# Another written-out order for all engines in a fused attention and feed-forward kernel

## The chip, the cores and the metric

One core of one Trainium2 chip runs the kernel. The metric is the device time of one execution in microseconds (us). TensorE is called PE here, ScalarE ACT, VectorE DVE, GpSimd POOL and SyncE SP, as in the profile.

## The reference, cut to what matters

Attention over 4 batches, 8 heads, 768 positions and 64 values per head. Some heads ("retrieval", three of eight here) see every earlier position; the others ("streaming") see the first 4 positions and a window of 64. Its result, 3072 tokens by 512, goes through a two-layer block with the activation h - tanh(h).

```
scores = q @ k.T / 8;  scores = where(mask, scores, -1e9)     # mask: causal, and per head full or sink + window
a = softmax(scores);   x = (a @ v), heads side by side         # x: 3072 x 512
h = x @ w_in                                                   # w_in: 512 x 2048
out = (h - tanh(h)) @ w_out                                    # w_out: 2048 x 512
```

Inputs and output are fp32; the kernel computes in fp16 with fp32 accumulation.

## The kernel before, in words

The tokens are cut into 12 tiles of 256 (`TT`); three tiles make a batch. A tile has four head pairs. For tile t and pair p the steps are: **T** t.p, four PE transposes that turn q and k of the pair (`st_T`, L1242), whose copies out of PSUM fill `QK` (L1222 on ACT, L1224 on DVE); **S**, the score products (`st_S`, L1367), numbered through by their PSUM area; **exp** on ACT (L1386); **mask pt**, a product on DVE (L1423); **A** t.p, the product with v (`st_A`, L1451); **rinv** and **x16**, reciprocal and scaling on DVE (L1471, L1512); **X** t.p, two PE transposes (L1547) and the copy **xT**. Tile 0 takes its masks as extra products ahead of S (**add**, L1340 and L1343). From tile 3 on, the transposes of q, k and x are done by DMA on SP's queue (`turn`, L750; `st_X_tile`, L1529), after POOL has gathered the heads in the order of their kind (`gather`, L848 and L884).

The second part runs in units. **H** t.u multiplies the tile's x by two column blocks of w_in (`H_unit`, L1598); units 0 and 1 need part 0 of w_in, 2 and 3 part 1, 4 and 5 part 2, 6 and 7 part 3. **th** t.u is the tanh on ACT (L1612), **gt** t.u the subtraction on DVE (L1623). **O** multiplies by w_out (L1671), from tile 4 on in a form with seven half-sized products instead of eight (`piece`, L1797), for which sums of operands are made on DVE or POOL (`sums`, L1764; `add`, L1868; `combine`).

For the early masks and products with far v, `masks` (L1094) and `scale_v` (L940: v times a per-head flag, one 128-row block of v each, called scale_v0 to scale_v3 for tile 0 and 1) make tables; `by_head` (L1082) makes the diagonal matrices for **add**; `by_rank` computes where each head goes, ending in `perm`, which POOL and DVE read into registers (`get`). The other loads of the start: `load_first` asks for q and k of tile 0, each in two halves of four heads, `cast_first` turns them into fp16; `load_cast(1)` brings q and k of tile 1 as fp16 through POOL's queue, and four **move** copies order them; `load_v`, `load_w_in` and `load_w_out` go through POOL's queue too, which casts on the way.

What sets the order: every operation is registered once with `P.op` in a fixed numbering, with its reads and writes. The list `SEQ`, written out in the source, is the order in which they are then issued; each engine gets its own operations in that order and works strictly in turn. `BANK` gives each PSUM user its bank. `SIZE` gives the lengths of filler matmuls (L2138: products of a matrix of ones, whose results nobody reads) that stand in PE's order at the start. `TE`, `XE`, `CASTS`, `IE`, `SUMS`, `ADDS`, `TAKES`, `SVS` and `OE` say which of two engines does a given copy, cast, sum or product.

```
for i in self.seq[a:b]:
    self.ops[i][2]()                     # Plan.follow: issue in the order of SEQ
```

Of the kernel before, what the change touches and what calls it, by code (L numbers as in the profile page):

```python
# [118 lines left out]
]  # L119
SIZE = {128: 20, 129: 17, 130: 7, 131: 6, 132: 3, 133: 11, 134: 6}  # L120


class Plan:
# [259 lines left out]
def kernel(  # L383
# [97 lines left out]
    XE = ('ADDA', 'AAAD', 'DADA')  # L481
# [6 lines left out]
    CASTS = ('AA', 'AD')  # L488
# [1828 lines left out]
```

## Time and profile before

| | |
|---|---|
| time, median of 3 runs | 222.72 us (222.02, 222.72, 224.2) |
| span of the profiled execution | 221.4 us; its whole time is not given beside it |
| PE busy | 212.2 us (96%) |
| DVE, ACT, POOL busy | 182.4, 136.2, 137.8 us |
| filler matmuls | 70, 6.6 us of PE's busy time |
| TensorE clock granted | 0.996 of full speed |

The span runs from the first to the last instruction of the program; the time of a run is a little longer. In a row of the timeline the columns are start, duration, engine, line, operation, tiles written and read, shape and count; brackets hold the idle time before it and what ended it. In a row of the windows, each engine has its busy time and its count of instructions in that stretch.

### The profile page before, as it was taken

The page shows a single profiled execution, that of the slowest core. Times are in us where ns is not written, and L with a number is a line of the kernel's source. Part 1 is how long each engine was busy: PE and PEld are TensorE (multiplying, and loading weights), DVE is VectorE, ACT ScalarE, POOL GpSimd, SP SyncE. Part 2 cuts the span into 40 slices and gives each one's busy share as a digit, 9 for nine tenths or more (in the row PEclk, how much of TensorE's full clock was granted, in tenths as well). Part 3 has the DMA queues.
Part 4 walks back from the last instruction along what each step waited for, and adds up shares of the span by engine and source line. Part 5 has one row for each costly group of instructions (what it writes and reads, how often), then busy time and mean ns, then how long its engine had stood idle before and what let it go on. Part 6 is the DMA issues. An engine that isn't in the chain of part 4 may idle for free. (4 is left out here: it accounts for less than half of the span.)

```text
span 221.4 us, 6599 instructions
## 1 busy us (share of the span) xinstructions
PE 212.2 (96%) x2485; PEld 175.6 (79%) x2485; DVE 182.4 (82%) x456; ACT 136.2 (62%) x223; POOL 137.8 (62%) x267
## 2 busy tenths in 40 slices
PE   7789999999999999999999999999999999999990
PEld 7467898788887576877887988989888888888880
DVE  5799976565959699899999999997887897786871
ACT  3779767995365869666475668546456865634510
POOL 8981993950757668489995798977985020071330
PEclk9999999999999999999999999999999999999998
DMA  6999999999999999999999988938137032022023
GB/s 174 172 197 206 144 177 157 191 235 190 199 200 218 239 192 201 217 193 256 209 266 202 213 160 171 236 63 132 49 69 172 3 95 98 3 47 96 3 96 104
DMA packets 112743, 34.56 MB, mean 156 GB/s; under 512 B 98882, under 2 KB 112194, under 8 KB 112706
## 3 DMA queue, kind: packets, MB, share of 16 engines
q1 hardware_dynamic: 86896, 26.75, 58.9%
q0 software_dynamic: 24992, 6.82, 30.2%
q10 hardware_dynamic: 818, 0.52, 0.8%
q8 instruction: 20, 0.33, 0.6%
q14 instruction: 17, 0.14, 0.2%
HBM read 27.26 MB, written 6.29 MB: 152 GB/s over the span
## 5 line engine op out<-in xcount | busy, mean ns | idle before, releaser
L1598 PE MATMUL banks<-xT,win 128*128 128x256 f16 x768 | 95.4, 273 | 0.1
L1612 ACT ACTIVATE th<-banks 128x512 f32<-128x512 f32 x96 | 55.4, 604 | 45.6 <-PE banks L1598 42.1
L1598 PEld LDWEIGHTS <-win 128*128 128x128 f16 x768 | 72.6, 98 | 11.7 <-issue 1.4
L1623 DVE SCALAR_TENSOR_TENSOR gt<-th,banks 128x512 f16<-128x512 f32 x88 | 58.0, 680 | 9.2 <-ACT th L1612 8.2
L1386 ACT ACTIVATE pt<-banks 128x1024 f16<-128x1024 f32 (+3 forms) x57 | 49.9, 911 | 6.4 <-PE banks L1367 6.1
L848 POOL CAST t<-rawqk 128x256 f16 x64 | 27.0, 448 | 15.6 <-DMA rawqk<-in_k_dram 10.4
L1797 PEld LDWEIGHTS <-m 128*128 128x128 f16 x256 | 24.4, 98 | 3.3 <-issue 0.4
L1671 PE MATMUL banks<-wout,gt 128*128 128x256 f16 (+1 forms) x160 | 26.1, 294 | 0.0
L884 POOL CAST v<-rawv 128x128 f16 x64 | 20.5, 350 | 6.8 <-DMA rawv<-in_v_dram 6.6
L1497 DVE TENSOR_TENSOR x16t<-banks,rinv 128x128 f32 (+1 forms) x80 | 22.9, 288 | 1.5
L1386 ACT ACTIVATE ptn<-banks 128x1024 f16<-128x1024 f32 (+1 forms) x18 | 17.2, 954 | 10.3 <-PE banks L1367 10.1
L1868 POOL TENSOR_TENSOR ot<-gu,ot 128x256 f32<-128x256 f32 x9 | 6.7, 744 | 24.5 <-ACT gu L1836 20.6
L1367 PE MATMUL banks<-QK 64*128 64x128 f16 (+1 forms) x343 | 21.1, 236 | 0.4 <-ACT pt L1386 0.3
L1797 PEld LDWEIGHTS <-gt 128*128 128x128 f16 x192 | 18.2, 98 | 2.9 <-issue 0.3
L1367 PEld LDWEIGHTS <-QK 64*128 64x128 f16 x343 | 13.0, 94 | 7.3 <-issue 6.1
L1451 PEld LDWEIGHTS <-pt 128*128 128x128 f16 x390 | 16.4, 97 | 1.7 <-issue 0.5
L1797 PE MATMUL banks<-wout,gt 128*128 128x256 f16 x128 | 17.8, 273 | 0.0
L1797 PE MATMUL banks<-wout,m 128*128 128x256 f16 x128 | 17.6, 273 | 0.0
L1671 PEld LDWEIGHTS <-gt 128*128 128x128 f16 x160 | 14.1, 98 | 3.9 <-issue 0.3
L1451 PE MATMUL banks<-v,pt 128*128 128x65 f16 x208 | 16.4, 193 | 0.0
L1471 DVE RECIPROCAL rinv<-banks 128x4 f32<-128x4 f32 x48 | 8.2, 175 | 7.0 <-PE banks L1451 6.9
L1423 DVE TENSOR_TENSOR pt<-pt,m4r 128x1024 f16<-128x1024 f16 (+1 forms) x18 | 12.7, 707 | 1.5 <-ACT pt L1386 1.3
(129 smaller groups left out, 324.6 us busy)
## 6 DMA issues: line engine op xcount, KB each, us to landing
rawqk<-in_q_dram SPq DMA_DIRECT2D x18, 256.0 KB, 4.3
out_dram<-ot SPq DMA_DIRECT2D x18, 256.0 KB, 2.6
rawqk<-in_k_dram SPq DMA_DIRECT2D x17, 256.0 KB, 4.3
rawv<-in_v_dram SPq DMA_DIRECT2D x16, 256.0 KB, 4.3
win<-in_moe_w_in_dram POOLq DMA_DIRECT2D x4, 512.0 KB, 8.9
wout<-in_moe_w_out_dram POOLq DMA_DIRECT2D x4, 512.0 KB, 9.4
out_dram<-ot SPq DMA_DIRECT2D x10, 128.0 KB, 4.1
v<-in_v_dram POOLq DMA_DIRECT2D x6, 128.0 KB, 6.7
```

The source lines that it names most:

```text
L848: nc.gpsimd.tensor_copy(out=c5()[:, :, :, s_ : s_ + 1, :], in_=r5()[:, :, :, at, :])
L884: nc.gpsimd.tensor_copy(out=v1s[b]()[:, g * NB : g * NB + NB, RANK[s_] : RANK[s_] + 1, 0:D], in_=rw()[:, :, at, :],)
L1367: nc.tensor.matmul(out=flat[:, 512 * hh + o : 512 * hh + o + nb * 128], lhsT=lhsT, rhs=QK[p_, hp, q_0 : q_0 + nb * 128], start=not added, ...
L1386: nc.scalar.activation(out=o_, in_=i_, func=AF.Exp, scale=inv_sqrt_d)
L1423: nc.vector.tensor_mul(out=pv, in0=pv, in1=m)
L1451: nc.tensor.matmul(out=av()[:, i, hh, :], lhsT=pt()[:, hh, co : co + 128], rhs=vv, start=(jb == first_jb[hh]), stop=(jb == qb),)
L1497: nc.vector.tensor_mul(out=xt()[:, :, at, :], in0=av()[:, :, hh : hh + 1, 0:D], in1=rinv()[:, :, hh : hh + 1].unsqueeze(3).to_broadcast([1 ...
L1598: nc.tensor.matmul(out=ph()[:, j, :], lhsT=w_in_t[fb // 4][:, cb, f0 : f0 + 128], rhs=xT()[:, :, cb, :], start=(cb == 0), stop=(cb == HP - 1),
L1612: lambda: nc.scalar.activation(out=th()[:], in_=ph()[:], func=AF.Tanh, scale=1.0 / XS),
L1623: nc.vector.scalar_tensor_tensor(out=o_, in0=a, scalar=-XS, in1=b, op0=ALU.mult, op1=ALU.add,)
L1671: nc.tensor.matmul(out=po()[:, c0:c1], lhsT=gt()[:, f, ts * 128 : ts * 128 + 128], rhs=w_out_t[:, f, c0:c1], start=(f == 0), stop=(f == NF ...
L1797: nc.tensor.matmul(out=po()[:, at : at + CM], lhsT=lhs(c), rhs=rhs(c), start=c == 0, stop=c == NC - 1,)
```

## The change

The arithmetic is the same. The numbers in `SEQ` stand in another order, `BANK` fits it, three fillers are left of seven, and 67 operations change their engine.

```diff
 SEQ = [
-    0, 1, 14, 7, 2, 4, 16, 10, 17, 3, 15, 5, 8, 6, 13, 18, 9, 19, 12, 57,
...
+    1, 3, 7, 15, 14, 4, 5, 6, 8, 9, 12, 13, 0, 18, 19, 128, 20, 10, 57, 37, 38, 21, 22, 49, 30, 35, 31,
...
-SIZE = {128: 20, 129: 17, 130: 7, 131: 6, 132: 3, 133: 11, 134: 6}
+SIZE = {128: 21, 129: 23, 130: 3}
-    TE = (('AA', 'AD', 'AD', 'AA'), ('AA', 'AA', 'DD', 'AA'), ('AA', 'AA', 'DD', 'DA'))
-    XE = ('ADDA', 'AAAD', 'DADA')
+    TE = (('AD', 'AA', 'DD', 'DA'), ('AA', 'DD', 'DA', 'AA'), ('AA', 'DA', 'DD', 'DD'))
+    XE = ('DDDA', 'DDAA', 'DADA')
-    CASTS = ('AA', 'AD')
+    CASTS = ('DA', 'AD')
-    SUMS = ('DDDDDDDD', 'DDDDDDDD', 'DDDDDDDD', 'DDDDDDDD', 'DDDDPPDP', 'PDDDDPDD', 'DDPDDDPP', 'DDDPDDPP', 'PDPDDPDP', 'DDDDDPDD', 'PDDDDPDD', 'DDPDDDDD')
+    SUMS = ('DDDDDDDD', 'DDDDDDDD', 'DDDDDDDD', 'DDDDDDDD', 'DDDDDPPP', 'DDDDPPPP', 'PDDDPPDP', 'DPPDPDPD', 'PDPDDPDP', 'PDDDPDDP', 'DPPPDDPD', 'DDDDDDPD')
...
-    SVS = ('PP', 'PP')
+    SVS = ('DD', 'DP')
-    IE = (('AD', 'DA'), ('DA', 'DA'))
+    IE = (('DD', 'DA'), ('DA', 'DA'))
-    OE = ('ADAD', 'AADD', 'AAAA', 'AAAA', 'AAAA', 'AAAA', 'AAAA')
+    OE = ('AAAA', 'DDDA', 'AAAA', 'AAAA', 'AAAA', 'AAAA', 'AAAA')
```

`ADDS` and `TAKES` change likewise. Read by names, the orders begin so (the two lists of an engine hold the same work, shifted):

```
SP before    load q half 0, load q half 1, load k half 0, two stores among raw loads of tile 4, turn 3, ...
SP after     load k half 0, load q half 0, load q half 1, two stores, turn 3, raw loads of tile 4, turn 3, ...
ACT before   load k half 1, cast q half 0, cast k half 0, cast q half 1, six QK copies, exp0, move, exp1, exp2, exp3, move
ACT after    load k half 1, cast k half 0, cast q half 1, q0.0, q0.1, k0.1, exp0, k0.3, exp1, exp2, move, exp3
POOL before  ..., load t1 q, v block 1, v block 0, load t1 k, v block 3, w_in 0, v block 2, w_in 1, w_in 2,
             scale_v0, table mS, scale_v3, scale_v1, w_in 3, table mS, registers (perm), w_out 0.0, tile 2, ..., w_out 0.1
POOL after   ..., load t1 q, v block 0, v block 1, load t1 k, w_in 0, w_in 1, v block 2, v block 3, w_in 2,
             tables mS, w_in 3, scale_v3, w_out 0.0, w_out 0.1, tile 2, tile 3, registers (perm), last q of tile 3, ...
DVE after    ..., by_head x4, cast q half 0, cast k half 1, by_head, k0.0, by_head, thr, mask, by_head, move, q0.2, k0.2, by_head,
             move, mask, q0.3, rinv0.0, x16 0.0, rflag0, move, mask, rinv0.1, rinv0.2, x16 0.1, xT0.0, x16 0.2, rinv0.3, x16 0.3,
             xT0.2, xT0.1, scale_v1, mask, q1.2, mask, k1.1, mask, q1.1, mask pt4, scale_v0, gt0.1, gt0.0, ..., by_rank spread to perm
PE before    fill x20, flags, fill x17, add 0, fill x7, T0.1, T0.0, T0.2, T0.3, fill x6, S 0, add 1, S 1, ..., S 3, A0.1, fill x3,
             X0.0, A0.2, T1.0, A0.2, A0.3, fill x11, X0.1, T1.3, T1.2, T1.1, X0.2, X0.3, fill x6, S 4, H0.0 and H0.1 in part, S 6
PE after     fill x21, flags, fill x23, T0.0, T0.1, add 0, T0.2, S 0, add 1, T0.3, S 1, A0.0, add 2, S 2, ..., S 3, X0.0, A0.2, T1.0,
             T1.3, fill x3, A0.3, X0.1, X0.2, T1.2, X0.3, T1.1, S 4, H0.0 and H0.1 whole, S 6
```

(S 0 to S 3 are tile 0; S 4, 6, 8 and 10 are the four pairs of tile 1, each with two PSUM areas, of which the second number is left out.)

In the diff's later part the order is shuffled for every engine to the end of the kernel: on SP the DMA transposes of tiles 4 to 8 stand at the same place or up to five places earlier, and loads of raw v stand later. The last seven operations of PE and the last six stores are the same.

More of the change, by code (lines that the diff above doesn't have):

```diff
@@ L499 @@
     STEPL = {1: (1, 4), 4: ('a',), 6: (2, 6, 'e'), 7: (5, 'b', 3, 7, 'f')}
-    SUMS = ('DDDDDDDD', 'DDDDDDDD', 'DDDDDDDD', 'DDDDDDDD', 'DDDDPPDP', 'PDDDDPDD', 'DDPDDDPP', 'DDDPDDPP', 'PDPDDPDP', 'DDDDDPDD', 'PDDDDPDD', 'DDPDDDDD')
-    ADDS = ('PPP', 'PPP', 'PPP', 'PPP', 'DDP', 'PDP', 'DPP', 'PPD', 'PPD', 'PPD', 'PPP', 'PPP')
-    TAKES = ('AA', 'AA', 'AA', 'AA', 'AA', 'DA', 'AA', 'AA', 'AA', 'AA', 'AA', 'AA')
-    SVS = ('PP', 'PP')
+    SUMS = ('DDDDDDDD', 'DDDDDDDD', 'DDDDDDDD', 'DDDDDDDD', 'DDDDDPPP', 'DDDDPPPP', 'PDDDPPDP', 'DPPDPDPD', 'PDPDDPDP', 'PDDDPDDP', 'DPPPDDPD', 'DDDDDDPD')
+    ADDS = ('PPP', 'PPP', 'PPP', 'PPP', 'PPD', 'PPD', 'PPD', 'DDP', 'PPD', 'DPP', 'DPP', 'PPP')
+    TAKES = ('AA', 'AA', 'AA', 'AA', 'AA', 'DD', 'AD', 'AA', 'AA', 'AA', 'AD', 'AA')
+    SVS = ('DD', 'DP')
     HINT = (11, 1, 0)
```

200 rows, old and new, of tables (BANK, SEQ) are left out of this document.

## The prediction, made before the changed kernel was run

> **What bounds the kernel now.** I read the page first, then PE by stages, then the timeline of the first 30 us, then the landings of single transfers.
>
> ```profile
> span 221.4 us, 6599 instructions
> PE 212.2 (96%) x2485; PEld 175.6 (79%) x2485; DVE 182.4 (82%) x456; ACT 136.2 (62%) x223; POOL 137.8 (62%) x267
> PE   7789999999999999999999999999999999999990
> ```
>
> PE is the only engine near its span, so the next question is where it isn't busy, or busy with nothing.
>
> ```profile
> 0.00:17.40 17.40, 13.82 (x177) 10.81 (x177) 13.29 (x43) 11.38 (x25) 14.63 (x27) 1.00 1.37 182
> 17.40:25.00 7.60, 7.32 (x103) 6.00 (x102) 7.25 (x23) 7.49 (x13) 3.90 (x6) 1.00 1.13 176
> 25.00:215.00 190.00, 189.70 (x2200) 157.93 (x2199) 160.00 (x387) 117.28 (x187) 118.63 (x234) 1.00 0.88 155
> 215.00:221.40 6.40, 1.36 (x13) 0.91 (x10) 1.82 (x7) 0.00 (x0) 0.68 (x2) 0.87 0.28 91
> L2138 PE MATMUL banks<-ones 128*128 128x128 f16 x70 | 6.6, 263 | 1.2 <-POOL ones L976 1.2
> PE banks L1367 <- DMA QK<-t: 0.2, 1, 0.2
> ```
>
> The windows give span, then busy time of PE, weight load, DVE, ACT, POOL. From 25 to 215 us PE is busy 189.70 of 190.00 us; its only wait there is 0.2 us. Nothing can be won there, only lost. The last 6.40 us hold the last results and stores, whose order is unchanged. What is left is the head: of its 17.4 us PE works 13.82, and 6.6 of these are fillers. So 10.2 us of the head (17.4 - 13.82 + 6.6) do nothing useful, and the change is worth what it takes from these, as far as PE stays fed afterwards. In the head I followed what each wait ended on:
>
> ```profile
> 3.91 0.62 ACT L1222 CAST t<-rawqk 128x512 f16<-128x512 f32 x1 [0.95 <-DMA rawqk<-in_q_dram]
> 5.99 0.43 DVE L1224 CAST t<-rawqk 128x512 f16<-128x512 f32 x1
> 6.87 1.14 ACT L1222 CAST t<-rawqk 128x512 f16<-128x512 f32 x2 [2.33 <-DMA rawqk<-in_k_dram]
> 7.54 1.14 PE L1242 MATMUL banks<-ident,t 128*128 128x128 f16 x14 [1.42 <-ACT t L1222]
> 8.38 0.45 DVE L1224 COPY QK<-banks 128x256 f16<-128x256 f16 x1 [1.36 <-ACT QK L1222]
> 9.69 0.87 ACT L1386 ACTIVATE pt<-banks 128x768 f16<-128x768 f32 x1
> 10.23 2.18 DVE L1094 TENSOR_SCALAR m<-A,thr 128x512 f16<-128x512 f16 x2
> 11.14 1.11 POOL L940 TENSOR_TENSOR vf<-v,rflag 128x520 f16<-128x520 f16 x1
> 12.70 2.11 POOL L940 TENSOR_TENSOR vf<-v,rflag 128x520 f16<-128x520 f16 x2
> 12.87 1.02 DVE L1224 COPY t<-t16p 128x512 f16<-128x512 f16 x1
> 15.88 0.42 DVE L1512 TENSOR_TENSOR x<-banks,rinv 128x256 f16<-128x256 f32 x1
> 17.41 1.50 PE L1598 MATMUL banks<-xT,win 128*128 128x256 f16 x12
> 18.34 0.35 DVE L1094 TENSOR_SCALAR m<-A,thr 128x512 f16<-128x512 f16 x1
> 18.85 0.56 PE L1367 MATMUL banks<-QK 64*128 64x256 f16 x10
> ```
>
> ACT waits 2.33 us for the first half of k, and PE 1.42 us behind it. From 8.38 us on DVE is the bound: it never rests, and it is slowed by POOL. A mask takes 0.35 us alone (18.34), but two take 2.18 where POOL's scale_v starts at 11.14, and a move takes 1.02 beside the scale_v of 12.70. The last x is ready at 16.3 us (15.88 + 0.42), the first H runs at 17.41.
>
> **The change part by part.** *k first.*
>
> ```profile
> L628 SPq DMA_DIRECT2D rawqk<-in_q_dram x1: 505/505/505, 1.4 to 1.4; - x1
> DMA to landing us min/median/max: 4.0/4.0/4.0
> rawqk<-in_k_dram ACTq DMA_DIRECT2D x1, 256.0 KB, 4.4
> ```
>
> SP's three loads land at 3.9, 5.4 (1.4 + 4.0) and 6.8 us; each wait above ended on one. They are of one size, so I give the same three times to k half 0, q half 0, q half 1. k half 1 on ACT's queue stays at 5.9 (5.99, cast). The first pair's transposes need q and k of half 0: 5.4 + 0.43 for DVE's cast is 5.9 us, against 7.54. But the cast of q half 1 stands on ACT ahead of the copies q0.0, q0.1, k0.1, so these wait for 6.8 + 0.6 = 7.5 us. exp0 then starts at about 8.4, against 9.69: of 1.6 us won at the transposes, 1.3 are left.
>
> *DVE's chain.* From its cast at 5.5 us to the last copy of x (xT0.1) DVE has 29 pieces in the new order: 2 casts and 5 QK copies of 0.43-0.45, 4 x16 of 0.42, 3 masks and 3 moves of 0.35 (bounds for a move 0.35 and 1.02; I take the low end, since no POOL product runs beside them), some 12 small ones of 0.16-0.3. That is about 9.5 us, less some overlap, plus waits for exp and PSUM: the end falls at 14.5 us, and at 15.5 if POOL's DMA issues slow the masks and moves. scale_v0 and scale_v1 now come behind that, on DVE. The trace has no such product on DVE; the nearest row above is POOL's 1.1, and a mask of 128x512 at 0.35 bounds it below; I take 0.7, in the middle. First H at 15.1 us (15.0 to 16.3).
>
> *What is late next.* The second S of tile 1 (18.85 above) waits for scale_v1, three masks and three QK copies that stand on DVE between xT0.1 and it: 0.7 + 3 x 0.35 + 3 x 0.43 = 3.0 us less overlap, so 17.1 us instead of 18.85. Ahead of it PE now does 16 H products instead of 12; four at 0.125 (1.50 for 12) are 0.5 more. **Lead there: 1.75 + 0.5 = 2.2 us**, or 0.3 if DVE's chain ends at its late bound and every piece after it is slowed too.
>
> *w_in sooner.*
>
> ```profile
> L815 POOL DMA_DIRECT2D win<-in_moe_w_in_dram x1: 780/780/780, 10.4 to 10.4; - x1
> DMA to landing us min/median/max: 10.7/10.7/10.7
> 22.35 1.16 PE L1598 MATMUL banks<-xT,win 128*128 128x256 f16 x9
> ```
>
> Part 2 is asked for at 10.4 and lands at 21.1, after 10.7 us of queue. Ahead of it stand the same eight loads as before, in another order. Parts 0 and 1 pass two blocks of v and come sooner, in time for 15.1 and 17.6; part 2 I leave at 21.1. PE would want it at 20.7 and waits 0.4. Its first use was at 22.35, and 0.66 us of H and X that stood behind it are now done before: **lead 1.25 + 0.66 = 1.9 us**.
>
> *w_out.*
>
> ```profile
> 21.10 0.90 POOL L826 DMA_DIRECT2D wout<-in_moe_w_out_dram  x1 [5.22 <-DVE gt L1623]
> L826 POOL DMA_DIRECT2D wout<-in_moe_w_out_dram x1: 902/902/902, 21.1 to 21.1; - x1
> DMA to landing us min/median/max: 6.2/6.2/6.2
> 28.21 0.38 PE L1671 MATMUL banks<-wout,gt 128*128 128x256 f16 x2
> ```
>
> Before, POOL stood 5.22 us at its register load ahead of w_out; part 0.0 landed at 27.3 (21.1 + 6.2), first use 28.21. The register load now stands behind 10 more DMAs, so POOL asks once v block 3 has landed and scale_v3 is done, near 19.8. Bounds: 26.0 (the same 6.2) and 27.3 (the queue as full as before). PE with its lead wants it at 26.6, and part 0.1, some 3 us behind it, at 29.8. Loss 0 to 1.1 us; I take 0.2, nearer the low end, since the 6.2 is the shortest wait of the large loads shown. **Lead 1.7 us.** The registers come late; POOL's gathers of tile 3 need raw data that land at 39 us, so 31 is early enough.
>
> *Keeping it to 215 us.*
>
> ```profile
> 84.82 2.90 SPq L1529 DMA_TRANSPOSE xT<-x16t  x1
> xT<-x16t SPq DMA_TRANSPOSE x1, 4.9
> 89.72 0.50 PE L1598 MATMUL banks<-xT,win 128*128 128x256 f16 x3
> ```
>
> This x landed at 89.7 (84.82 + 4.9) and PE used it at 89.72: no slack. A lead of 1.7 us lives on only if such transposes come 1.7 us earlier. In SP's new order this one has 37 operations ahead instead of 41, and those of tile 7 have 55 instead of 58; at 0.5 to 0.6 us for an issue that is about 2 us. Raw loads of v stand later for it, as tile 7 to 9 need them late. The moves between DVE and POOL cost nothing by themselves: from 25 us on DVE is busy 160.00 and POOL 118.63 of 190. Bounds: 0 and the whole lead. I take 0.
>
> *Fillers* are 47 instead of 70, in time that was idle.
>
> **Sum:** 221.4 - 1.7 = 219.7 us of span. The median of the runs stands 1.3 above the span of the profiled execution (222.72 - 221.4), which I keep: **221.0 us**. Less than 1%, 2.2 us, is about what can't be told from no change here.
>
> **Rivals.**
>
> *The whole lead arrives* (0.30): the queue isn't as full as I hold it, part 2 of w_in and w_out land with the earlier asking, and 2.2 to 3 us stay: 219.5 to 220.5, say 220.1. For it: part 0 of w_out, asked alone, took 6.2 us where part 2 of w_in took 10.7. Against it: the bytes ahead of part 2 are the same.
>
> *The lead is given back* (0.12): the x of tile 4 or the gathers behind more sums on POOL don't come sooner, PE waits there instead; 222.2, between 221.7 and 223.2. For it: slack zero at 89.72; against: those transposes were moved forward.
>
> *Slower* (0.11): POOL's register load waits for perm, whose small steps stand on DVE between eight subtractions of 0.7 us; behind it stand the last q of tile 3, v, and part 1.0 of w_out, which gates all later raw loads. Near 31 us it costs nothing. Each microsecond beyond moves tile 3 and then SP's whole queue; with the 1.7 us of lead used up at 34, a perm at 36.5 gives 225.2. Against it: DVE is, by the sum above, some 2 us ahead of its old pace then.
>
> *The clock* (0.05). Fillers ran before PE's real work, and there are 23 fewer in a head with gaps.
>
> ```profile
> 1.15 2.31 PE L2138 MATMUL banks<-ones 128*128 128x128 f16 x20 [1.15 <-POOL ones L976]
> 14.38 0.78 PE L2138 MATMUL banks<-ones 128*128 128x128 f16 x11
> ```
>
> The first twenty start 0.1 us apart (2.31 for 20), eleven later ones 0.06 (0.78 less 0.2 of drain); so PE speeds up on the way, though the granted clock reads 1.00 throughout, and it stayed fast over its 1.42 us of idling before 7.54. If the new gaps let it fall back to half pace for about 3 us of work, 1.5 us go: 222.5. The Trainium skill, page "TensorE: Matmul & The Clock Gate", section "What's actually happening", says that PE runs at half clock until a window of about 3.4 us was busy and falls back after an idle one. By that rule the new head, whose longest pause I put at 0.6 us, stays fast; the rows agree, and no run here shows a fall.
>
> A second rule speaks against the change: by the page "DMA: Bandwidth & Descriptors" of the Trainium skill, section "SWDGE vs HWDGE vs iDMA", POOL writes its descriptors into SBUF, from which DVE's two-port modes lock it out. A busier DVE beside POOL's ten issues would then make them later. [...]
>
> **How the numbers follow.** Forecast 0.42: 220.5 to 221.7, at 221.0. The rivals have 0.30, 0.12, 0.11 and 0.05. Faster by over 1% (under 220.5) is the whole lead and a little of the forecast's edge: 0.34. Slower by over 1% (over 224.9) is the register case: 0.10. The rest, 0.56, is within. The range runs from the low end of the whole lead, 219.5, past lead given back, to 223.4; it leaves out the slower case and some 0.05 below.
>
> **What would show it.** T0.0 near 6 us, exp0 near 8.4, first H near 15.1 with no wait for w_in, the S behind it at 17.1, waits of PE for win near 21 and for wout near 27, fillers 47, PE's busy time from 25 to 215 still over 189. I am wrong if masks and moves stay slow without POOL's products (then H starts after 16.3), if PE waits over 1 us in all between 25 and 215, or if POOL's register load ends after 34.

## The result, and the profile after

The changed kernel took **231.81 us** (median of 6 runs), the kernel before 223.41 in the same comparison: a ratio of 1.040, with a 95% interval of 1.034 to 1.046. The forecast was 221.0 us, with a range of 219.5 to 223.4. The first profile of the changed kernel is of a run with a lower clock (span 233.9 us, clock 0.98), and slower runs of that kind are left out of the ratios; so the lines here are from the profile of another run of the same kernel, after_again (span 230.2, clock 0.992; 231.0 us median against 222.47, ratio 1.038, 1.035 to 1.041), unless the text says otherwise. Lines of the source stand six further down than before (L1598 is L1604).

The page (busy times; the last row is PE in 40 slices) and the windows (PE, weight load, DVE, ACT, POOL):

```profile
span 230.2 us, 6542 instructions
PE 213.7 (93%) x2462; PEld 175.7 (76%) x2462; DVE 192.8 (84%) x463; ACT 133.7 (58%) x212; POOL 145.9 (63%) x271
PE   7979999998989999999789999999997999999990
```

```profile
0.00:17.40 17.40, 14.29 (x162) 11.35 (x163) 13.41 (x49) 10.62 (x20) 11.10 (x23) 1.00 1.36 183
25.00:215.00 190.00, 182.60 (x2122) 150.90 (x2119) 165.29 (x386) 114.58 (x181) 125.32 (x237) 1.00 0.91 151
```

From 25 to 215 us PE was busy 189.70 us before and 182.60 now: 7.1 us of the 8.8 that the span grew. The stretch in which nothing could be won is where it was lost. DVE is the line to look at: it is busy 192.8 us instead of 182.4, though eight sums of the second part went from it to POOL. PE's waits from 40 to 215 us:

```profile
PE banks L1457 <- DVE pt L1429: 1.7, 2, 1.4
PE banks L1604 <- DVE x16t L1503: 1.0, 1, 1.0
PE banks L1604 <- DMA xT<-x16t: 1.0, 1, 1.0
PE banks L1373 <- DMA QK<-t: 0.9, 1, 0.9
PE banks L1373 <- DVE ot L1862: 0.6, 1, 0.6
PE banks L1457 <- DVE ptn L1405: 0.6, 1, 0.6
```

Most end on DVE; the two that end on a transfer (DMA) stand at 53 and 67 us. One of them followed back, in the timelines of PE, DVE and POOL:

```profile
114.36 2.45 PE L1604 MATMUL banks<-xT,win 128*128 128x256 f16 x20 [1.03 <-DVE x16t L1503]
112.68 1.43 DVE L1717 TENSOR_TENSOR wout<-wout 128x256 f16<-128x256 f16 x1
114.03 0.28 DVE L1503 TENSOR_TENSOR x16t<-banks,rinv 128x128 f32 x1
111.67 1.15 POOL L1770 TENSOR_TENSOR m<-gt,m 128x512 f16<-128x512 f16 x1
112.78 0.51 POOL L909 TENSOR_TENSOR vf<-v,rflagr 128x195 f16<-128x195 f16 x1
113.23 0.74 POOL L854 CAST t<-rawqk 128x256 f16 x2
113.91 0.35 POOL L890 CAST v<-rawv 128x128 f16 x1
```

The sum of w_out at 112.68 is an instruction that took 0.28 us at its fastest in the kernel before. It took 1.43, while POOL ran one instruction after another without a pause; PE stood 1.03 us for the x16t behind it. The groups from 100 to 215 us show which instructions of DVE grow, first of before, then of the changed kernel (busy, mean ns):

```profile
L1423 DVE TENSOR_TENSOR pt<-pt,m4r 128x1024 f16<-128x1024 f16 x8 | 5.8, 726 | 0.6 <-ACT pt L1386 0.6
L1711 DVE TENSOR_TENSOR wout<-wout 128x256 f16<-128x256 f16 x8 | 3.0, 380 | 0.0
L1623 DVE SCALAR_TENSOR_TENSOR gt<-th,banks 128x512 f16<-128x512 f32 x56 | 37.1, 680 | 5.3 <-ACT th L1612 4.6
100.00:215.00 115.00, 114.84 (x1323) 99.83 (x1322) 100.93 (x229) 65.81 (x106) 68.96 (x123) 1.00 0.59 126
```

```profile
L1429 DVE TENSOR_TENSOR pt<-pt,m4r 128x1024 f16<-128x1024 f16 x8 | 8.1, 1025 | 0.0
L1717 DVE TENSOR_TENSOR wout<-wout 128x256 f16<-128x256 f16 x8 | 6.0, 765 | 0.0
L1629 DVE SCALAR_TENSOR_TENSOR gt<-th,banks 128x512 f16<-128x512 f32 x59 | 39.1, 677 | 5.6 <-ACT th L1618 5.3
100.00:215.00 115.00, 109.86 (x1260) 93.84 (x1259) 104.97 (x218) 65.42 (x103) 83.25 (x137) 1.00 0.63 130
```

Masks and sums of w_out, both of whose inputs lie in SBUF, grow from 726 to 1025 ns and from 380 to 765. gt, one of whose inputs lies in PSUM, stays (680 and 677). POOL is busy 83.25 us there instead of 68.96.

### The profile page after: what moved, and what is told of

The parts are those of the page before. It is cut to its first block, busy times and chain, and to the rows that moved or that the text cites. A ratio compares the mean times of both kernels' runs of the same rounds, so it can differ in the third digit from the quotient of the medians.

```text
span 233.9 us, 6542 instructions
## 1 busy us (share of the span) xinstructions
PE 215.6 (92%) x2462; PEld 176.2 (75%) x2462; DVE 196.1 (84%) x463; ACT 133.8 (57%) x212; POOL 144.9 (62%) x271
## 5 line engine op out<-in xcount | busy, mean ns | idle before, releaser
L1604 PE MATMUL banks<-xT,win 128*128 128x256 f16 x768 | 97.8, 276 | 2.0 <-ACT xT L1228 1.1
L1604 PEld LDWEIGHTS <-win 128*128 128x128 f16 x768 | 73.3, 99 | 14.0 <-issue 3.8
L854 POOL CAST t<-rawqk 128x256 f16 x64 | 27.5, 460 | 12.3 <-DMA rawqk<-in_q_dram 8.3
L1677 PE MATMUL banks<-wout,gt 128*128 128x256 f16 (+1 forms) x160 | 25.5, 294 | 0.0
L1503 DVE TENSOR_TENSOR x16t<-banks,rinv 128x128 f32 (+1 forms) x80 | 22.4, 287 | 1.4
L1392 ACT ACTIVATE ptn<-banks 128x1024 f16<-128x1024 f32 (+1 forms) x18 | 17.1, 953 | 10.7 <-DVE x16t L1503 5.3
L1770 POOL TENSOR_TENSOR m<-gt 128x512 f16<-128x512 f16 x13 | 15.6, 1209 | 4.3 <-DVE gt L1629 3.6
L1770 POOL TENSOR_TENSOR m<-gt,m 128x512 f16<-128x512 f16 x10 | 11.8, 1182 | 7.5 <-PE banks L1803 5.1
L1429 DVE TENSOR_TENSOR pt<-pt,m4r 128x1024 f16<-128x1024 f16 (+1 forms) x18 | 15.8, 880 | 0.3 <-ACT pt L1392 0.2
```

What stands on the lines that cost most here:

```text
L854: nc.gpsimd.tensor_copy(out=c5()[:, :, :, s_ : s_ + 1, :], in_=r5()[:, :, :, at, :])
L1392: nc.scalar.activation(out=o_, in_=i_, func=AF.Exp, scale=inv_sqrt_d)
L1503: nc.vector.tensor_mul(out=xt()[:, :, at, :], in0=av()[:, :, hh : hh + 1, 0:D], in1=rinv()[:, :, hh : hh + 1].unsqueeze(3).to_broadcast([1 ...
L1604: nc.tensor.matmul(out=ph()[:, j, :], lhsT=w_in_t[fb // 4][:, cb, f0 : f0 + 128], rhs=xT()[:, :, cb, :], start=(cb == 0), stop=(cb == HP - 1),
L1677: nc.tensor.matmul(out=po()[:, c0:c1], lhsT=gt()[:, f, ts * 128 : ts * 128 + 128], rhs=w_out_t[:, f, c0:c1], start=(f == 0), stop=(f == NF ...
L1770: lambda k=k, fn=fn, a=a, b=b, cs=cs, e=e: getattr(engs[e], fn)(out=S4[k][:, cs, :], in0=a()[:, cs, :], in1=b()[:, cs, :]),
```

## The experiments

The kernel before, measured beside them, took 222.3 to 223.5 us.

| run | time, us | ratio to before (95%) |
|---|---|---|
| after_again | 231.0 | 1.038 (1.035 to 1.041) |
| new_head | 225.9 | 1.013 (1.006 to 1.020) |
| new_tail | 234.1 | 1.047 (1.044 to 1.051) |
| new_from102 | 232.6 | 1.047 (1.044 to 1.050) |
| new_to97 | 232.2 | 1.040 (1.033 to 1.048) |
| after_old_sums | 235.3 to 243.7 | none: its four runs lie too far apart |
| before_new_sums | 227.3 | 1.022 (1.016 to 1.027) |
| after_short_sums | 227.0 | 1.024 (1.017 to 1.032) |
| after_memsets | 226.6 | 1.014 (1.006 to 1.021) |
| after_split_sums | 231.3 | 1.035 (1.022 to 1.048) |
| before_double_sums | 235.3 | 1.059 (1.051 to 1.067) |
| new_start | 226.8 | 1.016 (1.010 to 1.021) |

**Where it is lost.** The first profile of the changed kernel had one large wait, 5.4 us at 111 us, so the first theory put all on that place: raw v asked for late, and POOL's copies of it packed together (theory P). The same kernel was profiled again, and three kernels were spliced from both orders:

```diff
+SEQ = first 350 entries of the new order, then the rest as in the old    # new_head; new_tail the other way round
+SEQ = first 850 entries of the old order, then the rest as in the new    # new_from102
```

> The changed kernel once more, for a second profile. Theory P (port): POOL's copies of v come 10 to 24 us later than before and run without a pause from 102 to 115 us; DVE's sums of w_out, which read and write SBUF only, stand still beside them (3.29, 2.16 and 1.35 us instead of 0.28 to 0.5), and PE waits 5.4 us for a bank that DVE frees behind them. Expected: 231 to 232 us, a wait of PE of 4.5 to 6 us near 111 us and DVE's slow sums again. If the profile shows another place for the loss, theory P falls. Theory C (clock): the clock falls by itself and takes the time; then the granted clock and not the wait differs from run to run and a profile with clock 0.99 or more has no wait over 2 us.

> The new order of all engines up to 44 us, the old order (and the old choice of engines) from there. Theory P and theory O (the new order from 100 us on is bad in itself) both expect 222.8 us, since the 0.6 us that PE is ahead at 20 to 36 us stays and the wait at 111 us is gone. Theory H (the new head with fewer fillers, later registers and another w_out order does the harm) expects 231 us.

> The old order up to 44 us, the new order and choice of engines from there. Theories P and O expect the whole loss: 231 to 233 us, with a wait of PE of 4 to 6 us between 108 and 118 us. Theory H expects 222 to 224 us.

> The old order up to 102 us, so that all of the v of batch 2 (tiles 6 to 8) that POOL copied by then stays early; the new order and choice of engines from there. Theory P expects DVE's sums of w_out at under 0.7 us each and no wait of PE over 1 us near 111 us: 223 to 225.5 us, where up to 2.5 is the smaller loss that the changed kernel shows after 170 us. Theory O expects the wait of 4 to 6 us near 111 us all the same: 229 to 231 us.

The second profile showed 2.5 us in four waits between 112 and 119 us instead of one of 5.4, and others at 53, 66, 125, 128, 146 and 176 us. new_tail lost everything, so the loss needs the tail and not the head (theory H falls). new_head lost 3.5 us where I expected none. By the count of columns that is used for the head below, 1.0 of them were lost by 20 us, where its clock fell, and another 2.2 by 100 us. But new_from102, with the old early v, lost everything too:

```profile
PE banks L1457 <- POOL v L890: 3.6, 1, 3.6
```

PE waited there for a copy of v that stood behind two sums of 1.15 us on POOL. Theory P, as it stood, fell; what these kernels with the loss share is the new order and choice of engines after 102 us.

**The sums.** SUMS says which sums of `sums` POOL makes: 19 before, 27 after.

```diff
 after_old_sums     -    SUMS = (..., 'DDDDDPPP', 'DDDDPPPP', 'PDDDPPDP', ...)    # in the changed kernel
                    +    SUMS = (..., 'DDDDPPDP', 'PDDDDPDD', 'DDPDDDPP', ...)
 before_new_sums    the same line, the other way round, in the kernel before
 after_short_sums   +    if e == "POOL": cs = slice(cs.start, cs.start + 1)
 new_to97           +    SEQ = first 800 entries of the new order, then the rest as in the old
```

> The changed kernel with one line taken back: the choice of engine for the sums of the second part (SUMS), 19 on POOL as before instead of 27; the order stays. Theory S (POOL's eight more sums of 1.15 us keep POOL without pauses, and DVE's instructions that read and write SBUF only stretch beside them: DVE is busy 10.4 us more although it has eight sums fewer): DVE's busy time falls by several us although it gets eight sums more, PE's waits between 105 and 180 us shrink, 231 becomes 225 to 228 us. Theory O (the order itself, DVE being full): DVE gets 8 x 0.43 to 0.7 = 3.4 to 5.6 us more and the time rises to 233 to 236 us, or stays.

> The kernel before with the changed kernel's SUMS only: 27 sums on POOL instead of 19, order as before. Theory S: DVE's busy time rises or stays in spite of eight sums fewer, PE waits 1 to 4 us between 105 and 180: 224 to 227 us. Theory O: 222.5 us, no change.

> The changed kernel with every sum on POOL (27) done over a quarter of its columns, 128x128 instead of 128x512; the rest of these sums is left out. DVE has the same instructions as in the changed kernel. Theory S: POOL is some 20 us less busy, DVE's own instructions get shorter by several us in all, the waits of PE for DVE's mask (1.37 us near 176 us) and near 111 us go: 224 to 227 us. Theory O: the same waits stay, 230 to 231 us.

> The new order of all engines and the new choice of engines up to 97 us, the old one from there. Theories S and O: what is lost after 105 us in the changed kernel doesn't arise, 222.5 to 225 us, where the upper end has waits for late transfers at 50 to 70 us as in the second profile of the changed kernel (1.9 us). If the loss is prepared before 97 us by v asked for late (what is left of theory P): PE waits 3 us or more between 100 and 120 us and the time is 227 us or more.

In the old order the line alone costs 4.9 us. DVE was busy 186.3 us there, 3.9 more with eight sums fewer: masks 902 ns and sums of w_out 526 on average from 100 to 215 us, against 726 and 380. But the one long wait of PE, 1.94 us at 138.5, ended on an exp of ACT, and ACT had stood for an ot of POOL just before:

```profile
138.41 0.60 ACT L1836 ACTIVATE gu<-banks 128x512 f32<-128x512 f32 x1 [2.60 <-POOL ot L1868]
```

So in the old order POOL was late as well, and this run doesn't part the two. Taken back in the new order, the line doesn't help: the fastest of the four runs took 235.3 us, and in the profile, of a slower one, DVE with eight more sums was busy 194.9 us. My expectation of 225 to 228 us was wrong, and the 233 to 236 of theory O fits the fastest run. With the sums shortened, POOL was busy 124.6 us and DVE, with the very instructions of the changed kernel, 184.2 instead of 192.8; no wait of PE from 25 to 215 us was over 0.35 us. new_to97 came out against theories S and O, as I expected for what is left of theory P: POOL stood 4.0 us for raw v asked for late, and PE waited 1.4, 2.0 and 2.0 us between 100 and 121. A splice leaves work between two plans and can make waits of its own, so this doesn't show that late v costs anything in the changed kernel; it doesn't rule it out either.

**What of a sum does the harm:** that POOL works long, that it reads, or that its instruction is long?

```diff
 after_memsets       a POOL sum over 2 columns of each block (the rest is left out), then
                     +    2 x engs[e].memset(S4[k][:, cs, :], 0.0)
 after_split_sums    +    each POOL sum as two instructions over half of cs
 before_double_sums  +    each POOL sum made twice, in the kernel before
```

> The changed kernel with each of the 27 sums on POOL replaced: a sum over two columns of each block, which keeps its waits, and then two memsets over its 128x512, which write as much as the sum and read nothing; the rest of the sum is left out. POOL stays about as long busy for each (estimated 1.1 us from the memset of 128x128 at 0.20 and the smallest ones at 0.10). Theory S1 (DVE stretches because POOL reads SBUF beside it): DVE's instructions shorten as with the sums of a quarter, PE's waits near 111 and 176 us go, 225 to 228 us. Theory S2 (POOL is late: what it makes for others, the copies of q, k and v, comes 1.15 us later for each sum; or any work of POOL stretches DVE): 229.5 to 231.5 us, with the same waits.

> The changed kernel with each of the 27 sums on POOL made in two instructions over 128x256 instead of one over 128x512; the same is read and written, and the result is the same. It tells apart why the memsets helped: they read nothing (R), or they are two short instructions in place of a long one, so that DVE gets in between them (L). R: 230 to 232.5 us, DVE's masks of 128x1024 at about 1.0 us after 100 us as in the changed kernel (0.73 to 0.81 before, 0.76 with memsets). L: 225 to 228 us, masks at 0.75 to 0.85 us.

> The kernel before with each of its 19 sums on POOL done twice in a row: 19 x 1.15 = 22 us more work on POOL, nothing else changed. Theory S: DVE's busy time rises by 3 us or more though it has the same instructions, PE gets waits, 225 to 230 us. If only the order of the changed kernel makes POOL's load dear (rival): within 1 us of 222.4, and DVE's busy time stays at 182 to 184 us.

after_memsets: the page, DVE's groups from 100 to 215 us, and POOL's group of the memsets.

```profile
PE 213.6 (95%) x2462; PEld 175.2 (78%) x2462; DVE 183.8 (82%) x463; ACT 133.8 (60%) x212; POOL 146.0 (65%) x325
```

```profile
L1429 DVE TENSOR_TENSOR pt<-pt,m4r 128x1024 f16<-128x1024 f16 x8 | 6.0, 763 | 0.0
L1717 DVE TENSOR_TENSOR wout<-wout 128x256 f16<-128x256 f16 x8 | 3.1, 396 | 0.0
L1775 POOL MEMSET m<- 128x512 f16 x54 | 28.4, 525 | 3.1
```

POOL is as busy as in the changed kernel (146.0 and 145.9 us), but DVE is 9 us less busy with the same 463 instructions: masks 763 ns instead of 1025, sums of w_out 396 instead of 765. The time is 226.6 us, 1.014 of before instead of 1.038. So what stretches DVE isn't that POOL is busy, and the greater part of the loss isn't that POOL is late. after_split_sums, the same way:

```profile
PE 213.5 (93%) x2462; PEld 174.5 (76%) x2462; DVE 192.7 (84%) x463; ACT 133.5 (58%) x212; POOL 150.8 (66%) x298
```

```profile
L1429 DVE TENSOR_TENSOR pt<-pt,m4r 128x1024 f16<-128x1024 f16 x8 | 7.5, 946 | 0.0
L1717 DVE TENSOR_TENSOR wout<-wout 128x256 f16<-128x256 f16 x8 | 5.6, 711 | 0.0
L1771 POOL TENSOR_TENSOR m<-gt 128x256 f16<-128x256 f16 x26 | 19.2, 760 | 2.5 <-PE banks L1809 2.5
```

Shorter instructions that read as much help nothing: DVE 192.7 us, time 231.3. **It is POOL's reading of SBUF beside DVE's instructions with two inputs in SBUF.** The Trainium skill, page "SBUF — State Buffer", section "Who interferes with whom", states this: a DVE instruction with two SBUF inputs contends with a POOL instruction that reads SBUF, and not with one that only writes it. The three runs agree, and gt, with one input in PSUM, agrees too. The rows of the head go further than that sentence: the slow mask and the moves of 1.02 us beside scale_v have a single tensor input, in SBUF, and were held up all the same.

before_double_sums gives the dose in the old order: 19 more sums on POOL, DVE's instructions unchanged. Its page, and PE's waits from 100 to 215 us:

```profile
PE 216.1 (93%) x2485; PEld 176.5 (76%) x2485; DVE 189.8 (81%) x456; ACT 136.3 (58%) x223; POOL 163.8 (70%) x286
```

```profile
PE banks L1367 <- POOL kc L873: 3.4, 1, 3.4
PE banks L1800 <- POOL m L1765: 1.6, 2, 0.8
```

DVE was busy 7.4 us more, and the time rose by 11.8 us, more than the 225 to 230 expected: here POOL was late as well, as the waits on it show.

**The head.**

```diff
 new_start: first 200 entries of the new order (26 us), then the old; in it, on ACT
-    ..., q1.0, k1.2, xT0.3, ...
+    ..., q1.0, xT0.3, k1.2, ...
```

> The new order up to 26 us, the old order and choices from there, and in the new part one copy moved: ACT's copy of the last x of tile 0 (xT0.3) ahead of its copy k1.2. In the changed kernel PE's first H stops for 1.1 us since xT0.3 stands behind k1.2 on ACT, which waits 1.5 us for DVE's copy q1.2 of the same PSUM area. Expected if that is the place where the head's lead was lost: the wait of 1.1 us falls to 0.3 or less and PE is 1.5 to 2 us ahead of the kernel before at 20 to 24 us instead of 0.6 to 1.0. Whether the lead lives: if the transfers of 45 to 127 us follow, 220.5 to 221.5 us; if they are the bound (the x that landed with no slack at 89.7 us), 222 to 222.8 us.

The changed kernel's head in the timeline (two rows of PE, then of ACT); three rows of PE in new_start; and two rows of PE's waits in new_start from 18 to 100 us:

```profile
15.34 0.28 PE L1604 MATMUL banks<-xT,win 128*128 128x256 f16 x1
16.73 1.80 PE L1604 MATMUL banks<-xT,win 128*128 128x256 f16 x15 [1.11 <-ACT xT L1228]
15.99 0.44 ACT L1228 COPY QK<-banks 128x256 f16<-128x256 f16 x1 [1.50 <-DVE QK L1230]
16.30 0.38 ACT L1228 COPY xT<-banks 128x256 f16<-128x256 f16 x1
```

```profile
15.77 1.92 PE L1604 MATMUL banks<-xT,win 128*128 128x256 f16 x16
18.53 1.03 PE L1604 MATMUL banks<-xT,win 128*128 128x256 f16 x8 [0.32 <-ACT pt L1392]
20.21 0.19 PE L1457 MATMUL banks<-vf,pt 128*128 128x65 f16 x1 [0.65 <-ACT pt L1392]
```

```profile
PE banks L1553 <- DVE x L1518: 1.5, 1, 1.5
PE banks L1604 <- DMA xT<-x16t: 1.2, 1, 1.2
```

The 1.11 us went, as expected. Counted by the columns of all useful matmuls that PE had started by a time, at full pace, it was 1.8 us ahead of the kernel before at 18 us. At 24 us only 0.9 was left, as the next waits were for exp; then came 1.5 us for an x at 29 us and 1.2 for a transposed x at 91 us, and at 100 us it was 2.8 behind. The 226.8 us lie above both of my expectations; no lead lived.

## Why the prediction was wrong

**The step that failed is "Keeping it to 215 us"**, and in it the sentence that the moves between DVE and POOL cost nothing by themselves, since DVE was busy 160.00 and POOL 118.63 of 190 us. Both had room by their shares; but an instruction of DVE with two inputs in SBUF is held up while POOL reads SBUF, so where they meet, much of POOL's time is added to DVE's: 9.0 us of DVE's 192.8 went when POOL wrote instead of reading. The bounds that I gave that step, 0 and the whole lead of 1.7 us, left out what happened: 7.1 us of PE's time. My own rows had shown the two engines in each other's way, in the head: a mask at 1.9 us instead of 0.35 beside scale_v. I used it for scale_v alone and didn't carry it to the eight sums. The same step had the transposes come about 2 us sooner. With 37 operations ahead instead of 41, the one asked for at 84.82 was asked for at 84.38, and PE waited 0.97 us for another at 67 us.

**The head** was half right. Measured and forecast: first T 6.58 (6.0), exp0 8.87 (8.4), DVE's last copy of x done at 14.74 (14.5), first H 15.34 (15.1), fillers 47. Masks and moves without POOL's products took 0.28 to 0.67 us, near the low end that I chose, and scale_v on DVE 0.69 (0.7). But the step took DVE for the only carrier of x: XE gives the last copy, xT0.3, to ACT, where it came at 16.30, so that H stood still for 1.11 us and the second S of tile 1 came at 18.45 (17.1). The lead was 0.6 to 1.1 us at 20 to 36 us, not 1.7 to 2.2.

Even this lead isn't clear of the difference between executions. Four more profiles have the old head: new_tail, new_from102, before_new_sums and before_double_sums. By the same count of columns they were 0.1 to 1.0 us ahead of the profile of before at 20 us. In three of them POOL's scale_v met fewer of DVE's masks and moves, and the first H started at 16.0 to 16.4 us instead of 17.41. Three rows of before_new_sums:

```profile
12.50 0.29 DVE L1224 COPY t<-t16p 128x512 f16<-128x512 f16 x1
13.59 2.06 POOL L940 TENSOR_TENSOR vf<-v,rflag 128x520 f16<-128x520 f16 x2 [1.07 <-DMA v<-in_v_dram]
15.99 1.48 PE L1598 MATMUL banks<-xT,win 128*128 128x256 f16 x12
```

So the 17.41 from which I counted the lead was that of an execution on the late side (new_tail has 17.35), and much of what I meant to win from POOL's scale_v comes and goes in the old order by itself.

**w_in and w_out** held: part 2 of w_in landed at 21.21 (21.1), part 0.0 of w_out at 26.79 (26.0 to 27.3), and PE waited for neither. (The sum has PE want part 0.0 at 26.6; 28.21 less the lead of 1.9 is 26.3. Nothing hung on it.) **The register load** ended by 33.3 us, before the 34 from which I priced that rival; the slower outcome came by another mechanism, one I had not among the rivals.

**The clock** was priced at 1.5 us for a head with gaps. It fell, but elsewhere: behind the long waits. before_new_sums in windows around its wait at 138.5 us (the third column from the end is the granted clock):

```profile
138.50:140.50 2.00, 0.06 (x3) 0.03 (x2) 1.17 (x3) 2.00 (x4) 2.00 (x4) 1.00 1.10 228
140.50:142.50 2.00, 2.00 (x42) 1.92 (x42) 2.00 (x4) 1.21 (x2) 1.94 (x4) 0.79 1.15 256
142.50:144.50 2.00, 2.00 (x24) 1.66 (x22) 1.30 (x8) 1.09 (x2) 1.87 (x4) 0.50 1.06 306
144.50:146.50 2.00, 2.00 (x17) 1.70 (x16) 1.97 (x7) 0.45 (x1) 1.92 (x4) 0.86 0.37 86
```

By the same count of columns, PE fell back by 4.0 us between 130 and 150 us, where its only long wait was this one of 1.94. The idle window of about 3.4 us, by the rule that the prediction cites, was not needed for it. Nor was it right that no run showed a fall: the row of the last 6.40 us before, with its 0.87, showed one. In the head of new_head, with two pauses of 0.36 and 0.68 us, the clock did fall to 0.50 from 17 to 19 us; in the same head of after_again it did not.

**What stays open.** By the ratios the memsets win back 2.4 of the 3.8%. The other 1.4%, some 3 us, lies in several waits of 0.15 to 0.73 us in the profile of after_memsets, which no run took apart. new_head and new_start, without the new sums, lost about as much (1.3 and 1.6%), but whether by the same waits isn't shown. The two waits for late transfers in after_again (0.9 and 1.0) were not in the first profile, so they differ from execution to execution. Whether the later raw v adds to the loss wasn't separated: the loss came with early v (new_from102) and in new_to97 with a late one, both splices, and shrank with late v (after_memsets).

## What to carry to other kernels

Two engines with room by their busy shares may still hold one another up: before an operation moves from DVE to POOL, list which instructions of DVE with two inputs in SBUF run at that time, and price the case in which the times add up. Before a head is priced from one profile, see in a second one which of its waits come back. When the same instructions of an engine take longer after a change, compare their mean times by form, and keep one form with a PSUM input as the control. Where a table gives each copy its engine, follow the last one by its own engine's queue; it is the one that sets the start.

## What the runs showed of the hardware

One instruction of DVE can be held up past several of POOL: in the first profile of the changed kernel a sum of w_out took 3.29 us, while seven instructions of POOL began and ended beside it, four of which stand here in three lines. In new_tail one took 3.05 us.

```profile
108.66 3.29 DVE L1717 TENSOR_TENSOR wout<-wout 128x256 f16<-128x256 f16 x1
109.50 1.15 POOL L1770 TENSOR_TENSOR m<-gt,m 128x512 f16<-128x512 f16 x1
110.62 0.51 POOL L909 TENSOR_TENSOR vf<-v,rflagr 128x195 f16<-128x195 f16 x1
111.07 0.73 POOL L854 CAST t<-rawqk 128x256 f16 x2
```

And the clock fell to 0.50 behind a wait of PE of 1.94 us (before_new_sums), and did not behind one of 1.37 us (after_again, at 176 us). It is no simple threshold: in new_head it fell behind two pauses of 0.36 and 0.68 us.
